# A recurrence with a max-out layer: weight differences made in pairs of chunks, lower_bound loaded on ScalarE's queue, and the last pair of blocks as seven products

## The chip, the cores and the metric

The kernel runs on one core of one Trainium2 chip. The metric is the device time of an execution in microseconds (us). The profile's span is about 1.8 us shorter than the time of the same run, and the text says which one it means.

## The reference, cut to what matters

A gated recurrence over 4 sequences of 6144 tokens of width 256 is followed by a two-layer network whose hidden unit is the larger of two projections:

```python
f = lower_bound + (1 - lower_bound) * sigmoid(f_logit)
h = f[:, t] * h + (1 - f[:, t]) * x[:, t]         # t = 0 .. 6143, y[:, t] = h
g = np.maximum(y @ w1, y @ w2)                    # width 1024
out = g @ w_out                                   # width 256
```

All inputs and the output are float32.

## The kernel before: the parts that matter here

The maximum is `y@w1 + relu(y@(w2-w1))`, so TensorE (PE) makes one product with `wd = w2 - w1` per hidden chunk and folds `w1 @ w_out` into a small matrix `w13`. Tokens are worked on in 48 blocks of 512. From block 4 on, the second layers of two blocks are made together as seven half-size products instead of eight (a Strassen scheme, with sums of activations made by VectorE). In the kernel before, the last pair of blocks is an exception: it still runs the plain second layer.

At the start, everything has to be built once. SyncE (SP) issues the loads in this order, and VectorE (DVE) casts what arrives:

```python
nc.sync.dma_start(out=lbc[:], in_=lower_bound.rearrange("(h p) -> p h", p=P))
nc.vector.tensor_copy(out=ident[:], in_=ident_f[:])
nc.vector.tensor_scalar(out=om[:], in0=lbc[:], scalar1=-1.0, scalar2=1.0, ...)   # 1 - lower_bound
nc.vector.tensor_scalar_add(out=nom[:], in0=lbc[:], scalar1=-1.0)
fetch_first(0)          # first 256 rows of f and of x
fetch_first(1)          # the next 256 rows of each
for g in range(NG):
    fetch_w(g)          # half of w1, half of w2, 512 KB each
pool_waits(w1n[0][:, 0, 0:1])      # GpSimd (POOL) waits for the first weight piece ...
nc.gpsimd.dma_start(out=wob[:]...) # ... then loads w_out and the next chunks of f and x, casting them
```

wd is made a half (four chunks) at a time, and the transposed w1 is copied out between the halves:

```python
scale_w1(0); half_w1(0, nc.scalar.copy)
make_wd(0)                 # DVE: wd = om * w2 - w1s, 2 x [128 x 512]
pt = turn_w1(0)            # PE: transpositions of w1
keep_w1T(0, pt)            # DVE copies them out of PSUM
scale_w1(1)
for fc in range(4):
    first_layer(0, fc)     # PE: needs wd of chunk fc
# ... the same for half 1, chunks 4..7 ...
make_w13(0)                # PE: needs both transposed halves and wob
```

The kernel's end is the plain second layer of the last two blocks, 80 matmuls of 256 columns, where each 128-token group of the last block is evicted and stored by itself.

## Time and profile before

| | before |
|---|---|
| median of the first 3 runs (lowest to highest) | 380.85 us (380.81 to 381.16) |
| profiled run | 381.55 us, span 379.8 us |
| busy share of the span | PE 97%, VectorE 88%, ScalarE 79% |
| 16 DMA engines, 3 to 22 us | 90% busy or more, one short stretch aside (80%) |

The page's first lines and its chain of waits (shares of the span by engine, then by line) are:

```profile
PE 369.1 (97%) x4076; PEld 279.9 (74%) x4076; DVE 333.0 (88%) x402; ACT 300.3 (79%) x406; POOL 37.5 (10%) x79
...
PE 89%; DMA 4%; DVE 3%; POOL 1%; SPq 1%; ACT 0%; issue 0%
PE ps L605 42%; PE dT L436 41%; PE ps L482 6%; DMA xT<-in_x_dram 3%; DMA r<-in_moe_w_dram 1%; DVE r L230 1%; DVE S L506 1%; SPq L117 0%; PE ps L180 0%; DVE osb L496 0%; DVE v L223 0%; POOL fT L105 0%; DVE ff L213 0%; ACT r L444 0%; POOL wob L631 0%
```

PE is the limit nearly everywhere. The view of windows (stretch, its length, then busy us and instructions of each engine, the granted clock, the DMA share and GB/s) shows where it isn't:

```profile
0.00:12.50 12.50, 7.11 (x57) 5.60 (x57) 7.56 (x18) 7.38 (x12) 4.48 (x14) 1.00 0.84 266
...
67.00:350.00 283.00, 283.00 (x3310) 215.28 (x3309) 270.50 (x308) 239.19 (x328) 25.68 (x55) 1.00 1.02 211
350.00:366.90 16.90, 16.90 (x207) 13.15 (x205) 9.90 (x12) 12.28 (x15) 0.00 (x0) 1.00 0.16 64
366.90:380.00 13.10, 8.70 (x80) 7.71 (x78) 2.23 (x4) 1.33 (x3) 0.00 (x0) 1.00 0.42 162
```

From 67 to 366.9 us PE has no idle time at all. What PE does not fill lies in the first 25 us and in the last 13, but for 0.55 us between 25 and 67. The chain in order of time (start, length, what) shows what set PE's progress at the start, and the last pair at its end:

```profile
0.74 0.44 SPq L620
...
1.25 0.45 SPq L117
...
3.16 5.50 DMA r<-in_moe_w_dram
...
11.39 11.08 DMA xT<-in_x_dram
...
22.52 0.62 PE ps L180 x8
...
366.87 8.75 PE ps L482 x80
```

L620 is the load of lower_bound, L117 the first loads of f and x, `xT<-in_x_dram` is x of chunk 2 (counted from 0) by way of POOL, and L482 the plain second layer of the last pair.

### The profile page before, as it was taken

How to read it: one execution, taken by the hardware profiler on the slowest of the kernel's cores; microseconds unless marked ns; L12 is line 12 of the kernel's file. 1: busy time of each engine (PE TensorE's matmuls, PEld its weight loads, DVE VectorE, ACT ScalarE, POOL GpSimd, SP SyncE). 2: the span in 40 equal slices, each digit the busy share in tenths (PEclk: the TensorE clock that was granted, in tenths of full speed). 3: DMA queues.
4: the chain of work that ended last, by engine and by line, in shares of the span. 5: the costliest groups of instructions: out<-in, count | busy, mean ns of one | idle time of the engine just before them, and what ended most of it. 6: DMA issues, size and time to landing. Idle time of an engine off the chain costs nothing.

```text
span 379.8 us, 9454 instructions
## 1 busy us (share of the span) xinstructions
PE 369.1 (97%) x4076; PEld 279.9 (74%) x4076; DVE 333.0 (88%) x402; ACT 300.3 (79%) x406; POOL 37.5 (10%) x79
## 2 busy tenths in 40 slices
PE   4999999999999999999999999999999999999995
PEld 3677766777777777777777777777777777777784
DVE  4696789999999999999999999999999999999721
ACT  4846788798798888888888887987888888888740
POOL 1500103101201101102011011011011021000000
PEclk9999999999999999999999999999999999999999
DMA  7994999989999999999899999999999999970223
GB/s 249 242 226 98 265 162 256 167 156 289 195 195 276 180 190 251 202 172 285 143 257 190 219 251 278 127 263 223 182 263 212 188 268 211 192 265 3 110 113 113
DMA packets 103389, 77.17 MB, mean 203 GB/s; under 512 B 93554, under 2 KB 94066, under 8 KB 102642
## 3 DMA queue, kind: packets, MB, share of 16 engines
q1 hardware_dynamic: 100514, 51.13, 59.8%
q0 software_dynamic: 2544, 25.17, 34.5%
q8 instruction: 32, 0.52, 0.6%
q10 hardware_dynamic: 288, 0.26, 0.2%
q14 instruction: 11, 0.09, 0.1%
HBM read 53.48 MB, written 48.23 MB: 268 GB/s over the span
## 4 chain that ended last, share of the span: by engine, by line
PE 89%; DMA 4%; DVE 3%; POOL 1%; SPq 1%; ACT 0%; issue 0%
PE ps L605 42%; PE dT L436 41%; PE ps L482 6%; DMA xT<-in_x_dram 3%; DMA r<-in_moe_w_dram 1%; DVE r L230 1%; DVE S L506 1%; SPq L117 0%; PE ps L180 0%; DVE osb L496 0%; DVE v L223 0%; POOL fT L105 0%; DVE ff L213 0%; ACT r L444 0%; POOL wob L631 0%
## 5 line engine op out<-in xcount | busy, mean ns | idle before, releaser
L444 ACT ACTIVATE r<-dT 128x1024 f16<-128x1024 f32 x192 | 195.8, 1022 | 53.2 <-PE dT L436 53.0
L436 PE MATMUL dT<-r,wd 128*128 128x512 f16 x768 | 225.4, 379 | 1.0 <-DVE wd L360 0.5
L605 PEld LDWEIGHTS <-S 128*128 128x128 f16 x1680 | 110.9, 101 | 37.6 <-issue 0.6
L605 PEld LDWEIGHTS <-r 128*128 128x128 f16 x1260 | 87.3, 101 | 36.6
L230 DVE TENSOR_TENSOR_SCAN r<-ff,r,v 128x512 f16<-128x512 f16 x88 | 108.2, 1270 | 0.8
L605 PE MATMUL ps<-t,S 128*128 128x128 f16 x1260 | 97.8, 219 | 0.0
L436 PEld LDWEIGHTS <-wd 128*128 128x128 f16 x768 | 67.6, 113 | 6.4 <-DVE wd L360 1.1
L506 DVE TENSOR_TENSOR S<-r 128x2560 f16<-128x2560 f16 x42 | 62.4, 1485 | 10.1 <-ACT r L444 10.0
L605 PE MATMUL ps<-wob,r 128*128 128x128 f16 x672 | 67.4, 219 | 0.0
L506 DVE TENSOR_TENSOR S<-r,S 128x2560 f16<-128x2560 f16 x42 | 61.9, 1474 | 0.0
L285 ACT ACTIVATE u<-fT 128x512 f16<-128x512 f16 x88 | 56.0, 636 | 1.0 <-DMA fT<-scr 1.0
L213 DVE TENSOR_SCALAR ff<-u,nom 128x512 f16<-128x512 f16 (+1 forms) x98 | 31.3, 346 | 9.7 <-ACT u L207 5.3
L348 POOL CAST waited<-fT 128x1 f32<-128x1 f16 x21 | 10.8, 513 | 279.5 <-DMA fT<-scr 279.5
L605 PE MATMUL ps<-w,r 128*128 128x128 f16 x168 | 36.8, 219 | 0.0
L562 DVE TENSOR_TENSOR osb<-ps,sn 128x512 f32<-128x512 f32 x42 | 28.7, 684 | 6.8 <-ACT osb L560 5.3
L605 PE MATMUL ps<-t,r 128*128 128x128 f16 x420 | 33.4, 219 | 0.0
L605 PE MATMUL ps<-wob,S 128*128 128x128 f16 x336 | 31.4, 219 | 0.0
L223 DVE TENSOR_TENSOR v<-u,xT 128x1024 f16<-128x1024 f16 x44 | 30.1, 684 | 0.2 <-DMA xT<-scr 0.2
L482 PEld LDWEIGHTS <-r 128*128 128x128 f16 x240 | 23.9, 101 | 6.9
L482 PE MATMUL ps<-wob,r 128*128 128x256 f16 x192 | 26.8, 273 | 0.0
L550 ACT COPY sn<-ps 128x512 f32<-128x512 f32 x42 | 24.6, 587 | 1.1 <-PE ps L605 0.9
L560 ACT COPY osb<-ps 128x512 f32<-128x512 f32 x42 | 24.4, 582 | 0.5 <-PE ps L605 0.5
(56 smaller groups left out, 134.8 us busy)
## 6 DMA issues: line engine op xcount, KB each, us to landing
out_dram<-osb SPq DMA_DIRECT2D x47, 512.0 KB, 3.9
scr<-in_f_logit_dram POOLq DMA_DIRECT2D x22, 512.0 KB, 7.4
scr<-in_x_dram POOLq DMA_DIRECT2D x22, 512.0 KB, 10.4
r<-in_moe_w_dram SPq DMA_DIRECT2D x4, 512.0 KB, 6.8
fT<-in_f_logit_dram POOLq DMA_DIRECT2D x3, 256.0 KB, 9.2
xT<-in_x_dram POOLq DMA_DIRECT2D x3, 256.0 KB, 11.1
osb<-in_f_logit_dram SPq DMA_DIRECT2D x2, 256.0 KB, 4.5
osb<-in_x_dram SPq DMA_DIRECT2D x2, 256.0 KB, 4.1
```

What stands on the lines that cost most here:

```text
L213: nc.vector.tensor_scalar(out=ff[:, h, cols], in0=u[:, h, cols], scalar1=nom[:, h : h + 1], scalar2=1.0, op0=ALU.mult, op1=ALU.add,)
L223: nc.vector.tensor_tensor(out=like(v[:, :, cols], xT), in0=like(u[:, :, cols], xT), in1=xT, op=ALU.mult,)
L230: nc.vector.tensor_tensor_scan(out=y_of(j, h), data0=ff[:, h, o : o + TB], data1=v[:, h, o : o + TB], initial=0.0 if t0 == 0 else y_of(j - ...
L285: nc.scalar.activation(out=mids[p + NBLK, "u"][:, h, cols], in_=held[c, 0][:, h, cols], func=AF.Sigmoid, scale=-1.0,)
L436: nc.tensor.matmul(dT[:, fc % 2, :], lhsT=wd[:, kc, unit_cols(fc)], rhs=y_of(j, kc), start=(kc == 0), stop=(kc == KC - 1),)
L444: nc.scalar.activation(out=rts[j, k][:, g - 1 : g + 1, :].rearrange("p q (i m) -> p q i m", m=P), in_=dT[:].rearrange("p q (m i) -> p q i ...
L482: nc.tensor.matmul(ps[:, r, :], lhsT=left, rhs=right, start=(s == 0 and (r == 0 or j == NBLK - 1)), stop=(s == n - 1 and (r == 1 or j == N ...
L506: nc.vector.tensor_tensor(out=t[:], in0=a, in1=b, op=op)
L550: nc.scalar.copy(out=t[:], in_=bank[b][:])
L560: nc.scalar.copy(out=dst, in_=bank[b][:])
L562: nc.vector.tensor_tensor(out=dst, in0=bank[b][:], in1=snap[name][:], op=ALU.add)
L605: nc.tensor.matmul(bank[b][:, i, :], lhsT=a[:, k, cols], rhs=w, start=fresh, stop=after is not None, skip_group_check=True,)
```

## The change

Three parts, each meant to take something off an end of the kernel: wd is made for two chunks at a time, so that PE can begin the first layer sooner, and the copies of the transposed w1 move behind it; lower_bound is loaded on ScalarE's (ACT's) queue, so that SP's first load of f is issued sooner; and the last pair is made as seven products of 128 columns like all others, with its last product (the "M2" of the scheme) in two parts. With the second part go two small moves: ScalarE's first Sigmoid (`warm`) no longer needs lower_bound and runs earlier, and VectorE makes `nom` (lower_bound - 1) ahead of `om`. The core of the diff:

```diff
-    def make_wd(g):
+    def make_wd(g, pair):
+        def cut(t):
+            return t.rearrange("p (n q) -> p n q", q=NQ)[:, :, 2 * pair : 2 * pair + 2]
         for kc in range(KC):
             nc.vector.scalar_tensor_tensor(
-                out=wd[:, kc, g * NQ * P : (g + 1) * NQ * P],
-                in0=w2n[g][:, kc, :],
+                out=cut(wd[:, kc, g * NQ * P : (g + 1) * NQ * P]),
+                in0=cut(w2n[g][:, kc, :]),
 ...
-        nc.sync.dma_start(out=lbc[:], in_=lower_bound.rearrange("(h p) -> p h", p=P))
+        nc.scalar.dma_start(out=lbc[:], in_=lower_bound.rearrange("(h p) -> p h", p=P))
         nc.vector.tensor_copy(out=ident[:], in_=ident_f[:])
+        nc.scalar.activation(out=warm[:], in_=ident_f[:, 0:1], func=AF.Sigmoid)
+        nc.vector.tensor_scalar_add(out=nom[:], in0=lbc[:], scalar1=-1.0)
         nc.vector.tensor_scalar(out=om[:], in0=lbc[:], ...)
 ...
-        make_wd(0)
-        pt = turn_w1(0)
-        keep_w1T(0, pt)
         scale_w1(1)
-        for fc in range(4):
-            first_layer(0, fc)
+        pt0 = turn_w1(0)
+        for pair in range(2):
+            make_wd(0, pair)
+            for fc in range(2 * pair, 2 * pair + 2):
+                first_layer(0, fc)
 ...                                  # the same for half 1, then:
+        keep_w1T(0, pt0)
+        keep_w1T(1, pt1)
 ...                                  # the end: sum3 in the last round, then
-        for j in (NBLK - 2, NBLK - 1):
-            for slot in range(FC):
-                second_layer(j, slot)
+        sum1(p); sum2(p); sum4(p)
+        for step in sevenths(p):
+            step()
 ...                                  # in sevenths, for the last pair:
+            product("X", sub(3), given(t3))
+            then(leave_both("X"))    # DVE evicts X; ACT saves group 3 of X
+            product("E", sub(4), plain(1, hi))
+            then(leave("E", ja, hi, 2, True))
+            product("X", part(1, 1), given(t4), groups=range(3))
+            then(leave_last(slice(0, 3)))
+            product("Y", part(1, 1), given(t4), True, groups=range(3, 4))
+            then(leave_last(slice(3, 4)))
```

In the last pair every finished half (128 of the 256 columns) is stored at once, so a store there writes runs of 512 B, where the stores before wrote whole rows of 1 KB or four rows of 1 KB in one run.

More of the change, by code (lines that the diff above doesn't have):

```diff
@@ L356, in half_w1 @@
             copy(out=w1h[g][:, kc, :], in_=w1s[g][:, kc, :])
-    def make_wd(g):
+    def make_wd(g, pair):
+        def cut(t):
+            return t.rearrange("p (n q) -> p n q", q=NQ)[:, :, 2 * pair : 2 * pair + 2]
         for kc in range(KC):
             nc.vector.scalar_tensor_tensor(
-                out=wd[:, kc, g * NQ * P : (g + 1) * NQ * P],
-                in0=w2n[g][:, kc, :],
+                out=cut(wd[:, kc, g * NQ * P : (g + 1) * NQ * P]),
+                in0=cut(w2n[g][:, kc, :]),
                 scalar=om[:, kc : kc + 1],
-                in1=w1s[g][:, kc, :],
+                in1=cut(w1s[g][:, kc, :]),
                 op0=ALU.mult,
@@ L450, in first_layer, with store @@
             )
-    def store(j, osb, first=0, n=TB // P, queue=None):
+    def store(j, osb, groups=slice(0, TB // P), cols=slice(0, D), queue=None):
         b, t0, nb, c, o = blocks[j]
@@ L456, in store @@
             out=out[r0 : r0 + nb, :].rearrange("(p n) d -> p n d", p=P)[
-                :, first : first + n, :
+                :, groups, cols
             ],
-            in_=osb[:, first : first + n, :],
+            in_=osb[:, groups, cols],
         )
@@ L470, in second_layer @@
             g, r = divmod(i, 2)
-            if s == 0 and (r == 0 or j == NBLK - 1):
+            if s == 0 and r == 0:
                 acc["ps"] = ps_o.tile([P, 2, D], FP32, name="ps")
@@ L485, in second_layer @@
                 rhs=right,
-                start=(s == 0 and (r == 0 or j == NBLK - 1)),
-                stop=(s == n - 1 and (r == 1 or j == NBLK - 1)),
+                start=(s == 0 and r == 0),
+                stop=(s == n - 1 and r == 1),
                 skip_group_check=True,
             )
-            if j == NBLK - 1 and s == n - 1:
-                (nc.vector.tensor_copy if r else nc.scalar.copy)(
-                    out=osb[:, i : i + 1, :], in_=ps[:, r : r + 1, :]
-                )
-                store(j, osb, i, 1, nc.sync if r else nc.scalar)
-            elif r == 1 and s == n - 1:
+            if r == 1 and s == n - 1:
                 (nc.scalar.copy if j == 0 else nc.vector.tensor_copy)(
@@ L528, in sevenths, with product, open_bank @@
         ja, jb = 2 * p, 2 * p + 1
-        def product(b, left, w, fresh=False):
-            for i in range(TB // P):
+        end = p == NPAIR - 1
+        def product(b, left, w, fresh=False, groups=range(TB // P)):
+            for i in groups:
                 for k in range(KH + 1):
-                    steps.append([b, left, w(k), i, k, fresh and i == k == 0, None])
+                    new = fresh and i == groups[0] and k == 0
+                    steps.append([b, left, w(k), i, k, new, None])
         def then(fn):
             steps[-1][-1] = fn
-        def open_bank(b):
-            bank[b] = ps_o.tile([P, TB // P, P], FP32, name="ps")
+        def open_bank(b, i=0):
+            if i:
+                t = ps_d.tile([P, 2 * TB // P, P], FP32, name="dT")
+            else:
+                t = ps_o.tile([P, TB // P, P], FP32, name="ps")
+            bank[b] = t
         def seed(b, src):
@@ L564, in go, with leave_both, leave_last @@
                     )
-                if last:
+                if end:
+                    store(j, osbs[j], cols=cols)
+                elif last:
                     store(j, osbs[j])
+            return go
+        def leave_both(b):
+            def go():
+                leave(b, jb, hi, 5, False)()
+                t = snpool.tile([P, TB // P, P], FP32, name="sn")
+                nc.scalar.copy(out=t[:, 3, :], in_=bank[b][:, 3, :])
+                snap[4] = t
+            return go
+        def leave_last(at):
+            def go():
+                dst = osbs[jb][:, at, lo]
+                if at.start:
+                    nc.vector.tensor_tensor(
+                        out=dst, in0=bank["Y"][:, at, :], in1=snap[4][:, at, :],
+                        op=ALU.add,
+                    )
+                else:
+                    nc.scalar.copy(out=dst, in_=bank["X"][:, at, :])
+                store(jb, osbs[jb], at, lo, nc.sync if at.start else nc.scalar)
             return go
@@ L585, in sevenths @@
         then(snapshot("E", 5))
-        product("X", sub(2), given(t2))
-        then(snapshot("X", 2))
-        product("B", part(0, 1), plain(1, lo))
-        then(leave("B", ja, lo, None, False))
-        product("X", sub(3), given(t3))
-        then(leave("X", jb, hi, 5, False))
-        product("E", sub(4), plain(1, hi))
-        then(leave("E", ja, hi, 2, True))
-        product("X", part(1, 1), given(t4))
-        then(leave("X", jb, lo, None, True))
+        if end:
+            product("B", part(0, 1), plain(1, lo), groups=range(1))
+            product("X", sub(2), given(t2))
+            then(snapshot("X", 2))
+            product("B", part(0, 1), plain(1, lo), groups=range(1, 4))
+            then(leave("B", ja, lo, None, False))
+            product("X", sub(3), given(t3))
[6 more added lines that the diff above has]
+            then(leave_last(slice(3, 4)))
+        else:
+            product("X", sub(2), given(t2))
+            then(snapshot("X", 2))
+            product("B", part(0, 1), plain(1, lo))
+            then(leave("B", ja, lo, None, False))
+            product("X", sub(3), given(t3))
+            then(leave("X", jb, hi, 5, False))
+            product("E", sub(4), plain(1, hi))
+            then(leave("E", ja, hi, 2, True))
+            product("X", part(1, 1), given(t4))
+            then(leave("X", jb, lo, None, True))
         def runner(step):
@@ L601, in run @@
                 if fresh:
-                    open_bank(b)
+                    open_bank(b, i)
                 a = left()
@@ L624 @@
         )
-        nc.vector.tensor_scalar_add(out=nom[:], in0=lbc[:], scalar1=-1.0)
         fetch_first(0)
@@ L637 @@
                 fetch(c, s)
-        nc.scalar.activation(out=warm[:], in_=om[:, 0:1], func=AF.Sigmoid)
         wt = ps_d.tile([P, 2, 2 * TB], HALF, name="dT")
@@ L653 @@
         half_w1(0, nc.scalar.copy)
-        make_wd(0)
-        pt = turn_w1(0)
-        keep_w1T(0, pt)
         scale_w1(1)
-        for fc in range(4):
-            first_layer(0, fc)
-        half_w1(1, nc.vector.tensor_copy)
-        make_wd(1)
-        pt = turn_w1(1)
-        for fc in range(4, 8):
-            first_layer(0, fc)
-        keep_w1T(1, pt)
+        pt0 = turn_w1(0)
[3 more added lines that the diff above has]
+                first_layer(0, fc)
+        half_w1(1, nc.vector.tensor_copy)
+        pt1 = turn_w1(1)
+        for pair in range(2):
+            make_wd(1, pair)
+            for fc in range(4 + 2 * pair, 6 + 2 * pair):
+                first_layer(0, fc)
+        keep_w1T(0, pt0)
+        keep_w1T(1, pt1)
         steps = turn_steps(1)
@@ L715 @@
             more = p + 1 < NPAIR
-            seq = [(27, scans[p]["scan10"]), (36, scans[p]["scan11"])]
+            seq = [
+                (27, scans[p]["scan10"]),
+                (36, scans[p]["scan11"]),
+                (112, lambda: sum3(p)),
+            ]
             if more:
@@ L723 @@
                     (84, scans[p + 1]["scan01"]),
-                    (112, lambda: sum3(p)),
                     (131, scans[p + 1]["decay1"]),
@@ L753 @@
             step()
-        for j in (NBLK - 2, NBLK - 1):
-            for slot in range(FC):
-                second_layer(j, slot)
+        p = NPAIR - 1
+        sum1(p)
+        sum2(p)
+        sum4(p)
+        for step in sevenths(p):
+            step()
 _INS = ['x', 'f_logit', 'lower_bound', 'moe_w1', 'moe_w2', 'moe_w_out']
```

## The prediction

> **What bounds the kernel now.** The page gives PE 97% busy; the chain of waits puts 89% of the span on PE. The windows view has PE busy for all of 67 to 366.9 us, which the change doesn't touch. So the change is worth what its two ends are worth, out of 10.7 us that PE doesn't fill.
>
> **Start.** The chain of waits: from 0.74 us SP issues lower_bound (0.44 us), four 256 KB loads (0.45 us each), then the weights; the first weight piece lands at 8.66 and lets POOL issue; x of the third chunk lands at 22.47, and PE goes on at 22.52. The DMA view shows the 16 engines 90% busy or more from about 3 to 22 us (370 to 400 GB/s on weights, 205 on POOL's casting loads): a stream of fixed length that begins when SP gets to its first load.
> - lower_bound on ScalarE's queue takes 0.51 us from the front (1.25 to 0.74): the stream ends about 0.45 us earlier. The Trainium skill, "DMA: Bandwidth & Descriptors", section "Issuing engines are not separate DMA queues", says that another issuer saves issue time only; that is what is wanted here.
> - wd in pairs: wd takes 1.39 us per half on DVE, and the weight loads idle 0.55 us twice behind it. Pairs and a later keep_w1T (0.68 us) should end block 0's first layer near 15.6 instead of 16.83, but wob lands near 16.5 and that x at 22.47, so PE will wait longer there (0.3 to about 1 us). I give this part nothing of its own.
> From 51.4 to 64 us the chain is on DVE, but it starts from a PE result and moves along.
>
> **End.** The last pair is 80 matmuls of 256 columns, 8.75 us (109 ns each) after 366.87. Seven products are 140 of 128 columns at 55.5 ns (27 took 1.51 us): 7.8 us. The last relu ends at 366.42; a sum takes 1.48 us (1.40 pipelined), so sum1 is ready at 368.0, just when product 1 ends, sum2 at 369.4, sum4 at 370.8. PE should end near 374.75, not 375.61. The last eviction is 128x128, about 0.3 us against 0.42. Stores become half rows of 512 B: packets took 45 ns for 1 KB, 84 for 2, 159 for 4, so I estimate 26 ns; the same page (Specifications) puts the line-rate minimum at 512 B, so no collapse. The last two stores (256 KB) need about 0.8 us of engines from 375.8, against 0.5 us from 376.9. Last byte about 376.65 against 377.4: 0.75 us gained. The 2.4 us from there to the end of the span stay.
>
> **Sum.** 0.45 + 0.75 = 1.2 us: 379.6 us, range 379.0 to 380.3. Chances: faster by over 2% 0.01, within 2% 0.98, slower 0.01.
>
> **Right or wrong.** Right if the first load is issued at about 0.74; x of chunk 2 lands about 0.5 us earlier; PE waits for it about 1 us, is busy from there to about 1.3 us before its old end, and shows no gap over 0.1 us in the last products; 512 B packets take about 26 ns.
>
> **What would make it wrong.** lower_bound's 4-byte packets still delaying the first load; the table load behind ScalarE's issue delaying the first sigmoid; 512 B packets as slow as 1 KB ones, or half-row stores issuing slower than 0.33 us; sums late on DVE; strided wd halves costing clearly more than half.

## The result, and the profile after

| | before | after |
|---|---|---|
| median (lowest to highest), 4 runs each | 380.83 us (380.80 to 381.16) | 380.18 us (380.08 to 380.82) |
| ratio of the fast runs | | 0.9985, 95% interval 0.9967 to 1.0002 |
| span of the profiled run | 379.8 us | 378.5 us |

Ratios here are the mean time of one kernel's fast runs over that of the other's of the same rounds, so they are not quite the ratio of the medians. The medians differ by 0.65 us. The forecast was 379.6 us with a range of 379.0 to 380.3, so the range holds, but the gain is about half of the 1.2 us that I summed up. The two spans differ by 1.3 us, which looks like my sum; but the span of before came from a slow draw. Against a second profile of the kernel before (b_again below, span 378.97 us) the change's 378.50 is 0.47 us shorter: 0.39 of it before the first layer of block 1, 0.08 from the last pair on.

The page after:

```profile
PE 367.7 (97%) x4136; PEld 279.2 (74%) x4136; DVE 338.4 (89%) x409; ACT 302.4 (80%) x410; POOL 36.2 (10%) x79
...
PE 92%; DVE 5%; DMA 1%; ACT 0%; issue 0%; DVEq 0%
```

The chain after, in order of time:

```profile
0.74 3.87 DMA lbc<-in_lower_bound_dram
4.63 0.17 DVE nom L667
...
4.87 0.34 DVE nat L128
...
11.32 0.39 DVE wd L365
11.75 2.10 PE dT L441 x8
```

This is not the chain I had forecast. The stream of loads is gone from it. It now begins with lower_bound itself, which takes 3.87 us to land, and VectorE's first cast of f (L128) stands behind the two operations on it. From there it runs over VectorE to wd and on to PE. The wait for x of chunk 2, which should have grown to 1 us, isn't there at all.

The end, as the timeline of the kernel before and that of the kernel after show it (start, length, engine, line, operation; in brackets the idle time before it and what ended it). Before:

```profile
374.57 1.04 PE L482 MATMUL ps<-wob,r 128*128 128x256 f16 x8
...
375.64 0.42 DVE L491 COPY osb<-ps 128x256 f32<-128x256 f32 x1 [1.76 <-PE ps L482]
```

After:

```profile
366.82 1.13 PEld L649 LDWEIGHTS <-S 128*128 128x128 f16 x20 [0.17 <-DVE S L506]
...
372.37 0.22 PE L649 MATMUL ps<-w,S 128*128 128x128 f16 x1
...
372.61 1.00 PE L649 MATMUL ps<-t,r 128*128 128x128 f16 x15
...
373.44 0.44 PE L649 MATMUL dT<-t,r 128*128 128x128 f16 x5
...
373.99 0.29 DVE L589 TENSOR_TENSOR osb<-dT,sn 128x128 f32<-128x128 f32 x1 [0.68 <-PE dT L649]
374.15 0.43 ACTq L460 DMA_DIRECT2D out_dram<-osb  x1
```

From the start of the last pair's first matmul to the end of the last, PE took 8.90 us before (366.71 to 375.61) and 8.36 after (365.52 to 373.88): 0.54 us gained, not 0.86. Two gaps of 0.18 us show: before the second product, which waits for sum1, and before the last, where the starts of two neighbouring matmuls are 0.24 us apart instead of 0.056, because VectorE (until 372.25 us) and then ScalarE (until 372.56) first have to read the bank that it adds to.

### The profile page after: what moved, and what is told of

The parts are those of the page before. It is cut to its first block, busy times and chain, and to the rows that moved or that the text cites. A ratio compares the mean times of both kernels' runs of the same rounds, so it can differ in the third digit from the quotient of the medians.

```text
span 378.5 us, 9591 instructions
## 1 busy us (share of the span) xinstructions
PE 367.7 (97%) x4136; PEld 279.2 (74%) x4136; DVE 338.4 (89%) x409; ACT 302.4 (80%) x410; POOL 36.2 (10%) x79
## 4 chain that ended last, share of the span: by engine, by line
PE 92%; DVE 5%; DMA 1%; ACT 0%; issue 0%; DVEq 0%
PE ps L649 45%; PE dT L441 42%; PE ps L487 4%; DVE r L230 1%; DVE S L506 1%; DMA lbc<-in_lower_bound_dram 1%; PE ps L180 1%; DVE v L223 1%; DVE r L264 1%; DVE ff L213 0%; PE ps L397 0%; DVE osb L496 0%; ACT r L449 0%; PE ps L137 0%; ACT u L258 0%
## 5 line engine op out<-in xcount | busy, mean ns | idle before, releaser
L649 PEld LDWEIGHTS <-S 128*128 128x128 f16 x1760 | 115.4, 101 | 37.8 <-issue 0.6
L649 PEld LDWEIGHTS <-r 128*128 128x128 f16 x1320 | 90.9, 101 | 36.7
L649 PE MATMUL ps<-t,S 128*128 128x128 f16 x1320 | 101.6, 219 | 0.0
L506 DVE TENSOR_TENSOR S<-r 128x2560 f16<-128x2560 f16 x44 | 65.4, 1487 | 14.4 <-ACT r L449 14.3
L649 PE MATMUL ps<-wob,r 128*128 128x128 f16 x704 | 69.9, 219 | 0.0
L506 DVE TENSOR_TENSOR S<-r,S 128x2560 f16<-128x2560 f16 x44 | 65.0, 1478 | 0.0
L649 PE MATMUL ps<-w,r 128*128 128x128 f16 x176 | 38.5, 219 | 0.0
L348 POOL CAST waited<-fT 128x1 f32<-128x1 f16 x21 | 9.4, 449 | 280.6 <-DMA fT<-scr 280.6
L568 DVE TENSOR_TENSOR osb<-ps,sn 128x512 f32<-128x512 f32 x44 | 30.1, 685 | 3.2 <-PE ps L649 3.2
L487 PEld LDWEIGHTS <-r 128*128 128x128 f16 x160 | 16.0, 101 | 6.2
L649 PE MATMUL ps<-w,S 128*128 128x128 f16 x88 | 19.3, 219 | 0.0
```

What stands on the lines that cost most here:

```text
L487: nc.tensor.matmul(ps[:, r, :], lhsT=left, rhs=right, start=(s == 0 and r == 0), stop=(s == n - 1 and r == 1), skip_group_check=True,)
L506: nc.vector.tensor_tensor(out=t[:], in0=a, in1=b, op=op)
L568: nc.vector.tensor_tensor(out=dst, in0=bank[b][:], in1=snap[name][:], op=ALU.add)
L649: nc.tensor.matmul(bank[b][:, i, :], lhsT=a[:, k, cols], rhs=w, start=fresh, stop=after is not None, skip_group_check=True,)
```

## The experiments

Twelve kernels were run, in three groups of four. Each was timed against the kernel before in the same rounds, and each left a profile. Each group ran on another chip, so times are set against the kernel before of their own rounds. All gave correct results.

One reading of the profiles orders everything. Let "first layer of block 1" be the start of PE's first matmul of that stage. From there to the first matmul of the last pair it is 341.54 or 341.55 us in ten of these profiles with the stage order unchanged and one core clock, before or after, whichever parts they have. The window view shows the same stretch with the same PE busy time. The kernel before (its second profile, b_again):

```profile
24.40:365.90 341.50, 340.95 (x3830) 257.04 (x3828) 314.54 (x368) 284.67 (x382) 34.07 (x61) 1.00 0.96 201
```

The kernel after:

```profile
24.00:365.50 341.50, 340.95 (x3830) 257.02 (x3828) 316.18 (x370) 284.48 (x382) 28.63 (x61) 1.00 0.96 202
```

So a span is the start, plus 341.55, plus the end, and each part of the change can be read from two numbers. This table is worked out from the profiles' instruction and packet times (us):

```
profile     1st decay  wd starts  w13 starts  1st layer  last pair to  span
            on DVE     on DVE     on PE       block 1    end of span
before      5.76       11.09      16.67       25.16      13.06         379.77
b_again     5.77       10.78      16.36       24.36      13.06         378.97
lb_only     6.34       11.03      16.61       24.62      13.11         379.26
wd_only     5.81       10.61      15.40       23.43      13.06         378.03
tail_only   5.86       10.75      16.57       24.90      12.96         379.40
after       6.53       11.23      15.94       23.97      12.98         378.50
no_lb       5.84       10.89      15.60       24.22      12.96         378.72
nom_late    6.20       11.03      16.25       24.65      12.96         379.16
full_rows   6.34       11.04      15.75       23.78      13.02         378.35
lb_rows     5.28       10.45      17.70       25.70      12.99         380.24
turn_late   5.81       10.86      16.13       24.14      12.96         378.77
rows_late   5.33       10.76      16.34       24.41      13.01         379.08
rows_gate   5.33       10.44      15.49       23.89      12.99         378.87
```

And the times:

| run | parts | median (lowest to highest) | ratio to before | 95% interval |
|---|---|---|---|---|
| after | all three | 380.18 (380.08 to 380.82) | 0.9985 | 0.9967 to 1.0002 |
| b_again | none | 380.76 (380.66 to 381.14) | 0.9995 | 0.9982 to 1.0008 |
| lb_only | lower_bound | 381.14 (380.98 to 381.38) | 1.0003 | 0.9990 to 1.0016 |
| wd_only | wd in pairs | 380.60 (379.81 to 380.98) | 0.9985 | 0.9972 to 0.9999 |
| tail_only | seven products | 380.80 (380.49 to 381.44) | 0.9995 | 0.9982 to 1.0009 |
| no_lb | wd and seven products | 379.96 (379.66 to 380.53) | 0.9975 | 0.9961 to 0.9988 |
| nom_late | all, VectorE reordered | 380.32 (379.78 to 380.94) | 0.9984 | 0.9970 to 0.9999 |
| full_rows | all, whole-row stores | 380.63 (380.13 to 381.15) | 0.9993 | 0.9978 to 1.0008 |
| lb_rows | all, lower_bound as rows | 381.27 (379.07 to 382.27) | 0.9999 | 0.9974 to 1.0025 |
| turn_late | no_lb, one stage moved | 380.83 (379.88 to 382.41) | 1.0001 | 0.9984 to 1.0018 |
| rows_late | lb_rows, one stage moved | 380.86 (380.12 to 381.26) | 0.9997 | 0.9984 to 1.0010 |
| rows_gate | rows_late, POOL later | 380.58 (379.92 to 380.65) | 0.9987 | 0.9975 to 0.9999 |

lb_third isn't in the tables; it stands below. The kernel before ran 42 times in all, its first profiled run not counted: median 380.85, 380.52 to 382.35, 8 of 10 between 380.64 and 381.36. Differences of a few tenths are therefore read from the profiles, and the times are only asked whether they agree. A profile is one draw too: after and full_rows have the same start, word for word, and their wd starts 0.19 us apart (11.23 and 11.04).

### The kernel before, profiled again (b_again)

No edit. Theory A held that the first profile had been a slow draw; the rival was that the change made POOL's loads faster.

> The kernel before, unchanged, for a second profile. The profiled run of before was 0.7 us over that kernel's median, and there POOL's loads of the start were slow (the wob load was waited for until 16.53 us, against 14.84 in the profile after). Theory A (that profile was a slow draw of the start): x of chunk 2 now lands before about 21.9 us, PE doesn't wait for it, and PE reaches the last pair's products about 0.7 us earlier, near 366.2 us instead of 366.87. Rival B (the change itself made POOL's loads faster): x of chunk 2 lands near 22.5 us again. Ratio 1.000 either way.

PE's transposition of x of chunk 2 began at 21.74 us without a wait, and the last pair at 365.91. Theory A holds: this profile is 0.8 us shorter than the first one of the same kernel, all of it before block 1's first layer. Its chain at the start does not run over the stream at all:

```profile
2.21 4.17 DMA osb<-in_f_logit_dram
...
10.14 0.73 DVE r L264
10.87 1.31 DVE wd L360 x2
12.17 0.60 DVE w1T L384
12.77 0.67 DVE S L356 x2
13.44 1.33 DVE wd L360 x2
14.82 1.70 PE dT L436 x7
16.52 0.87 PE ps L392 x8
```

In this execution, whose time is at the kernel's median, the start is a chain on VectorE: the first recurrence, the first half of wd, the copy of the transposed w1 (L384), a cast, and the second half of wd, with PE behind. That copy and those halves are what the wd part of the change cuts.

### lower_bound alone (lb_only)

```diff
-        nc.sync.dma_start(out=lbc[:], in_=lower_bound...)
+        nc.scalar.dma_start(out=lbc[:], in_=lower_bound...)
+        nc.scalar.activation(out=warm[:], in_=ident_f[:, 0:1], func=AF.Sigmoid)   # was behind om
         # nom ahead of om
```

> Only lower_bound on ScalarE's queue (with the early warm-up and nom ahead of om). My prediction's step: SP's stream starts 0.51 us earlier and PE with it: 0.45 us faster. Theory A: VectorE, in order, waits for lower_bound until about 4.6 us because its 4-byte packets now share the engines with the 2 KB packets of the first loads, so the first cast starts at about 4.8 us instead of 4.0 and the first recurrence ends no earlier: within 0.2 us of before, or slower by up to 0.5.

It gained nothing: 381.14 us at the median against 380.75 for before in the same rounds, with an interval that holds 1. VectorE in b_again:

```profile
2.88 0.17 DVE L622 TENSOR_SCALAR om<-lbc 128x2 f32<-128x2 f32 x1 [1.31 <-DMA lbc<-in_lower_bound_dram]
...
5.77 0.48 DVE L213 TENSOR_SCALAR ff<-u,nom 128x256 f16<-128x256 f16 x2
```

VectorE in lb_only:

```profile
4.44 0.17 DVE L623 TENSOR_SCALAR nom<-lbc 128x2 f32<-128x2 f32 x1 [2.88 <-DMA lbc<-in_lower_bound_dram]
...
6.34 0.48 DVE L213 TENSOR_SCALAR ff<-u,nom 128x256 f16<-128x256 f16 x2 [0.78 <-ACT u L258]
```

lower_bound lands 1.56 us later than when it goes first on SP, although it is issued at the same 0.74 us. The first decay starts 0.57 us later and wd 0.25 us later. Theory A holds. One step of my prediction also holds: the first piece of the weights does land earlier. POOL sees the first weight piece landed at 8.15 to 8.30 us in the four profiles with lower_bound on ScalarE's queue as 4-byte packets, and at 8.43 to 8.89 in the six with it first on SP. It did not help here, because VectorE's chain, which starts from f and x, was the longer one.

The packets of the trace say why lower_bound lands late. Counted from them, in each quarter of a microsecond: KB of f, x and weights whose transfer started, and the number of 4-byte packets (lower_bound is 256 of them; the rest are semaphores):

```
from us   b_again       after         lb_rows
1.75        0 KB  59     26 KB   0     28 KB   0
2.25        8 KB  96     38 KB   0     52 KB   0
2.75       46 KB   0     54 KB  43     92 KB   5
3.00       84 KB   0     30 KB  65     96 KB   5
3.25       92 KB   4     14 KB  82     94 KB   4
3.50       60 KB  12     18 KB  36     70 KB  10
3.75       54 KB   0     18 KB  21     70 KB   2
4.00       84 KB   3     12 KB  39     54 KB   6
4.25       74 KB   8     84 KB   2     40 KB   3
```

First on SP, lower_bound's packets run at a time when the engines have nothing else: the first of them starts at 1.82 us in b_again. On ScalarE's queue the first one starts at 2.82 us (2.49 to 2.82 in the four profiles with it there, though it is issued as early), which is part of the late landing and stays unexplained. From then on they run beside the first loads, and from 3.0 to 4.25 us the loads start 92 KB (128 to 162 in the other three) where b_again's start 374. The 0.5 us of head start is spent there. The Trainium skill, "DMA: Bandwidth & Descriptors", section "Queues, rings and completion order", says that each engine takes turns between the queue rows that have work; that fits packets of two queues mixing for a whole microsecond, but by the packets' own durations (9 ns) they should have cost little.

### wd in pairs alone (wd_only)

The edit is the `make_wd` part of the diff above with the order of the calls, and nothing else.

> Only wd in pairs of chunks, with keep_w1T behind. My prediction's step: nothing, PE waits longer for x of chunk 2. Theory A: in a usual run that x lands early enough, so that the first layer of block 0 ends about 1.0 us earlier and PE reaches the second layer 0.7 to 1.1 us earlier: 0.6 to 1.1 us faster.

The profile agrees with Theory A (0.93 us at block 1's first layer), but it is that of the fastest of the six runs (379.81), set against a median run of b_again. The ratio, 0.9985, is that of the whole change: about 0.57 us, with an interval from 0.04 to 1.07. The median of the runs moved only 0.15 us. PE in b_again:

```profile
11.57 2.37 PE L436 MATMUL dT<-r,wd 128*128 128x512 f16 x8
...
14.22 0.38 PE L436 MATMUL dT<-r,wd 128*128 128x512 f16 x1
14.82 1.70 PE L436 MATMUL dT<-r,wd 128*128 128x512 f16 x7 [0.23 <-DVE wd L360]
16.36 1.04 PE L392 MATMUL ps<-wob,w1T 128*128 128x256 f16 x8
```

PE in wd_only:

```profile
11.38 1.89 PE L441 MATMUL dT<-r,wd 128*128 128x512 f16 x8
...
13.55 2.01 PE L441 MATMUL dT<-r,wd 128*128 128x512 f16 x8
15.40 1.06 PE L397 MATMUL ps<-wob,w1T 128*128 128x256 f16 x8
```

The cleanest measure is the distance from the first wd operation to the first product of w13 (L392, L397), because it leaves out when the first loads came. It is 5.58 us in before, b_again and lb_only, and 4.79, 4.71, 4.71 and 4.71 in wd_only, after, no_lb and full_rows: 0.8 to 0.9 us. In the other profiles it is longer, and the gain is in part waited away: with pairs 5.05 in rows_gate, 5.22 in nom_late, 5.27 in turn_late, 5.58 in rows_late and 7.25 in lb_rows, and without them 5.82 in tail_only. Two reasons show in the traces: w1 turned late (tail_only's first layer began 1.25 us after wd, b_again's 0.79) and TensorE at full rate late (see lb_rows below). A third, wob late, is likely in nom_late: the product, which reads wob, began 0.28 us behind its turn there, and POOL saw wob land at 16.49. I had given this part nothing. It is where the gain of the start comes from.

### The last pair as seven products alone (tail_only)

The edit is the part of the diff from `store` to `sevenths`, with the last lines of the kernel.

> Only the last pair as seven products, with half-row stores. My prediction's step: 0.75 us faster. Theory A, from the profile after: PE ends the last pair in 8.2 us instead of 8.74 (0.54 gained, with two gaps of 0.18 us), but from the end of PE to the end of the span it takes 4.6 us instead of 4.2: 0.0 to 0.2 us faster.

From the last pair's first matmul to the end of the span it took 12.96 us, against 13.06: 0.1 us, as Theory A had it, and no measurable time (380.80 against 380.75). PE's gain of half a microsecond is given back behind PE. In b_again the last byte is written 2.11 us after the last matmul starts, in after 2.84 us. Counted from the last pair's first matmul, the last byte even comes later than before: 10.98 us in after and 10.97 here, 10.72 in before and b_again. That the span still ends 0.1 us sooner is due to the time behind the last byte, which I can't explain (full_rows below). The DMA view of the end lists the stores (line, queue, count, size, median us from issue to landing); before (b_again):

```profile
out_dram<-osb ACTq DMA_DIRECT2D x2, 128.0 KB, 2.5
out_dram<-osb SPq DMA_DIRECT2D x2, 128.0 KB, 2.1
```

After:

```profile
out_dram<-osb SPq DMA_DIRECT2D x3, 256.0 KB, 2.6
out_dram<-osb ACTq DMA_DIRECT2D x1, 192.0 KB, 2.8
out_dram<-osb SPq DMA_DIRECT2D x1, 64.0 KB, 2.4
```

The packets of 512 B took 25 to 26 ns, as I had estimated from the three larger sizes in the trace of the kernel before. But the store with 512 of them took 1.29 us from issue to its first packet where the engines were idle (371.05 to 372.34), and I had reckoned with the 0.80 of a store with 128. The five stores of the last pair then follow each other almost without a pause, from 372.34 to 376.50.

### The change without lower_bound's part (no_lb)

```diff
-        nc.scalar.dma_start(out=lbc[:], in_=lower_bound...)
+        nc.sync.dma_start(out=lbc[:], in_=lower_bound...)     # first, as before; warm and om as before
```

> The change without its lower_bound part: wd in pairs and the seven products, lower_bound first on SP again. Theory A (wd pairs gain about 0.6 to 0.9 us, the tail about 0.1, lower_bound on ScalarE's queue loses about 0.3): 0.7 to 1.0 us faster than before, and 0.2 to 0.4 faster than the whole change; PE reaches the last pair near 365.0 us instead of 365.5. Rival (the gain of the whole change needs the earlier first load): no faster than the whole change.

379.96 us at the median, 0.90 below before in the same rounds, ratio 0.9975 with an interval that ends at 0.9988. It is the fastest of the kernels by median, and the only one whose interval lies clearly below 1. Its profile is that of its slowest run (380.53): PE waited for x of chunk 2 there,

```profile
21.58 0.62 PE L180 MATMUL ps<-ident,xT 128*128 128x128 f16 x8 [0.42 <-DMA xT<-in_x_dram]
```

so that the last pair came at 365.77 and not near 365.0; that number of Theory A missed in this draw. Against the whole change the runs are 0.2 us better at the median (379.96 and 380.18), but from other rounds and with overlapping intervals, so it is shown only that the lower_bound part isn't needed for the gain.

### VectorE doesn't wait for lower_bound (nom_late)

```diff
-        nc.vector.tensor_scalar_add(out=nom[:], in0=lbc[:], ...)   # and om
         ...
         first_bf16(0, 0, nc.vector.tensor_copy)
         first_bf16(0, 1, nc.vector.tensor_copy)
+        nc.vector.tensor_scalar_add(out=nom[:], in0=lbc[:], ...)   # and om
```

The Trainium skill, "TensorE: Matmul & The Clock Gate", gives VectorE's queue as strictly first in, first out (its table of specifications), and the chain after shows it: the cast of f stands behind nom. This run asks how much that wait costs by itself.

> The whole change, with VectorE's two operations on lower_bound put behind its first two casts. It keeps the slowed stream (the 4-byte packets among the 2 KB packets from 3 to 4 us) and takes away VectorE's in-order wait for lower_bound. If that wait is what costs: the first cast starts near 4.2 us instead of 4.8, the first decay near 5.9 instead of 6.5, PE reaches the last pair 0.4 to 0.6 us earlier than the whole change. If the slowed stream is what costs: the second cast still waits for x until about 5.4 us and PE gains under 0.2 us.

The first cast moved to 4.18 us, as expected of the wait, but the cast of x still waited for its data until 5.58, as expected of the slowed stream. The first decay came at 6.20 (after: 6.53, b_again: 5.77) and wd at 11.03 (11.23 and 10.78). So the slowed stream is what costs most. What the wait in order adds is not settled: full_rows keeps it and drew 6.34 and 11.04, so between nothing and 0.2 us is left at wd. The time, 380.32, is that of the whole change; wob landed late in this draw.

### lower_bound without 4-byte packets (lb_rows)

```diff
-        nc.scalar.dma_start(out=lbc[:], in_=lower_bound.rearrange("(h p) -> p h", p=P))
+        nc.scalar.dma_start(out=lbr[:], in_=lower_bound.rearrange("(h p) -> h p", p=P))   # 2 rows of 512 B
 ...
+        nc.tensor.transpose(lbt[:], lbr[:], ident_f[0:KC, 0:KC])
+        # nom and om from lbt, behind the two casts
```

> The whole change, with lower_bound loaded as two rows of 512 B on ScalarE's queue, turned by one fp32 transposition on PE, and nom and om made behind the first two casts. No 4-byte packets are left in the start. If these slowed the stream: from 3 to 4 us the engines start over 80 KB per 0.25 us instead of 14 to 30, f lands before 3.6 us and x near 4.7 instead of 5.4, and PE reaches the last pair 0.3 to 0.6 us earlier than with lower_bound first on SP (no_lb): 1.0 to 1.5 us faster than before. If not: x lands near 5.2 us again and the result is that of no_lb.

The cause was hit and the gain was not. With two packets in place of 256 the loads run at 92 to 96 KB per quarter microsecond from 2.75 to 3.5 us (the table above), f is cast at 3.52 and x at 4.14 us, and the first decay starts at 5.28, half a microsecond ahead of b_again. That settles that the 4-byte packets slowed the stream. But the runs went from 379.07, the fastest of all, to 382.27, and the profile, taken of a slow one (382.05), shows the weights late. ScalarE in lb_rows:

```profile
9.01 1.34 ACT L352 ACTIVATE r<-r,om 128x512 f32<-128x512 f32 x2 [1.11 <-DMA r<-in_moe_w_dram]
10.26 1.13 ACT L356 CAST S<-r 128x512 f16<-128x512 f32 x2
```

The scaling of w1 (L352) had to wait 1.11 us for its data; in after it starts at 8.22 without a wait. PE turns w1 before it begins the first layer, so in this draw the first layer waited for w1 (ScalarE's casts, done at 11.4 us) and not for wd, which had started at 10.45. A second chain, weights to ScalarE to PE, lies close behind the VectorE chain, and shortening one by half a microsecond brings up the other.

That is only half of this draw's loss. The first layer of block 0 also ran slowly. PE in lb_rows:

```profile
12.16 3.52 PE L441 MATMUL dT<-r,wd 128*128 128x512 f16 x8
...
15.97 1.89 PE L441 MATMUL dT<-r,wd 128*128 128x512 f16 x8
```

The first eight matmuls start 0.427 us apart, the next eight 0.216, the same form with no wait between them. The trace's record of the clock that TensorE is granted, at its full share (1.0), begins at 15.46 us here, just where the spacing halves; in the other twelve profiles of the table it begins between 9.37 and 13.20. From the first layer's first matmul to w13 it took 5.54 us, against 4.02 in wd_only (lines above): 1.5 us of TensorE's rate, beside about 1 us of waiting for w1. The same shows in smaller measure in rows_late (about 0.75 us, full rate at 13.20), and in nom_late and turn_late (0.3 to 0.4 us, at 12.59 and 12.61). Why the full rate came late in these draws is not shown, nor whether it spreads the runs that left no trace.

### lower_bound third on SP's own queue (lb_third)

As nom_late, with lower_bound issued by SP between the first x and the second f.

> As nom_late, but lower_bound is issued on SP, third, behind the first f and x, so that its 4-byte packets share a ring with the 2 KB packets and not a second ring beside it. Theory A1 (4-byte packets cost wherever they run beside loads): the engines start under 40 KB per 0.25 us for about 1 us again, x lands near 5.2 us or later. Theory A2 (only the turn-taking between two rings costs): the 4-byte packets pass in a burst behind x, f lands near 3.5 us and x near 4.2, the first decay starts near 5.3 us, and the second halves of f and x land about 0.5 us later than in nom_late or the same.

The profile fell in the slow state (granted clock 0.95 from 11.07 us on, where its record begins), so only its first microseconds are used. f was cast at 3.63, x at 4.30, and the first decay started at 5.38 us: Theory A2. The 4-byte packets passed in a burst, 253 of them from 3.5 to 4.0 us. The place mattered: on the same queue behind x they delay neither f nor x. But the second halves of f and x came later (second decay at 8.98 us, 8.63 in nom_late), and the fast runs lay between 379.66 and 382.09 us: no gain.

### Whole rows at the end (full_rows)

```diff
-                if end:
-                    store(j, osbs[j], cols=cols)
-                elif last:
+                if last:
                     store(j, osbs[j])
 ...
-                store(jb, osbs[jb], at, lo, ...)
+                store(jb, osbs[jb], at, ...)          # groups 0 to 2 and group 3, all 256 columns
```

> The whole change, with the last pair stored in whole rows: the first block of the pair at once behind its last product, the second in one piece of 3 KB and one of 1 KB per partition. In the profile after, a half-row store of 3 or 4 pieces per partition takes 1.26 to 1.29 us from issue to its first byte, against 0.80 for one piece. Theory A: these take 0.80 us again, but 0.5 MB more waits for the end, so that the last byte is within 0.3 us of the whole change's and the time is the same. My prediction's step (half rows carry less at the end and cost nothing else): 0.4 to 0.6 us slower than the whole change.

Both expectations are half right. The first store's first packet came 0.83 us after its issue again (373.19 to 374.02), but the last two waited behind it, and the last byte came 11.51 us after the last pair's first matmul, against 10.98 in after: 0.53 later, as my prediction's reckoning of bytes has it. Yet the span ended 13.02 us after that matmul, against 12.98. So the form of the stores is worth 0.04 us in these two profiles, and the time from the last byte to the end is not fixed, as I had assumed: 2.3 us in before, 2.0 in after, 1.5 here. What sets it stays open.

### Three attempts to make the start robust (turn_late, rows_late, rows_gate)

```diff
         for fc in range(FC):
-            if fc == 4:
-                turn(turn_steps(2))
-                gate(2)
             second_layer(0, fc)
+        turn(turn_steps(2))
+        gate(2)
-        pool_waits(w1n[0][:, 0, 0:1])          # rows_gate only
+        pool_waits(w2n[0][:, 0, 0:1])
```

turn_late is no_lb with this move, rows_late lb_rows with it, and rows_gate adds the later start of POOL.

> As no_lb (wd in pairs, seven products, lower_bound first on SP), with the transpositions of block 2 moved behind the whole second layer of block 0, 2.2 us of PE later. In no_lb's profile PE waited for x of chunk 2 (0.42 us, until 21.58) in that draw. If POOL's late landings are what spreads the runs: no wait for that x in any draw, PE reaches the last pair at 365.0 us or earlier, median 0.2 to 0.5 us below no_lb's and a narrower spread. If the order costs VectorE its slack: the scans of block 2 start about 1.4 us later and PE waits for them at the first layer of block 2, no gain.

> As lb_rows (lower_bound as two 512 B rows), with block 2's transpositions moved as in turn_late. lb_rows ran between 379.07 and 382.27; its profile was a slow draw (382.05) in which f and x were ready 0.5 to 1.0 us early, but the weights came late: from 10.5 to 11.8 us, when POOL's wob packets had begun, the engines started 12 to 68 KB per 0.25 us. If only the late x of chunk 2 cost it: 379.0 to 379.8 in every run. If the late weights cost it (PE's first layer of block 0): again runs over 381.

> As rows_late, with POOL's first load held back until the second weight piece has landed instead of the first, so that its packets meet less of the weights' stream. If that collision makes lb_rows's slow runs: no run over 380.5 us, the weights' last packets end by 12.0 us, and the median is near 379.3. If not: the same spread as lb_rows.

None beat no_lb. In its profile the move took away the wait for x of chunk 2, and it cost 0.12 us later (341.67 us in the middle). turn_late still spread from 379.88 to 382.41, so that wait is hardly what spreads the runs. rows_gate did part of what its theory expects: the weights' last packet ended at 11.71 us (12.03 in rows_late, 12.52 in lb_rows), no run was over 380.65 us, and w13 started at 15.49 in its profile, where TensorE was also at full rate by 11.43 us. But it lost 0.44 us in the middle (341.99), and its median is 380.58, not 379.3: holding POOL back gives the gain away again. Five runs don't show that it narrows the spread.

## Why the prediction was right or wrong

The range was right, and so was the statement that the change is worth what its two ends are worth: the middle is 341.54 to 341.55 us in all profiles that keep its order. But the sum was right only by errors that cancel.

- "A stream of fixed length that begins when SP gets to its first load ... the stream ends about 0.45 us earlier": this step failed. The first load was issued at 0.74 us as forecast, and the first weight piece did land earlier, by about 0.4 us. But lower_bound's packets, moved out of an empty stretch into the busy one, slowed f and x, and VectorE stood behind lower_bound; alone, this part put block 1's first layer 0.26 us later in the profile (a difference that two draws of one start can also have) and gained nothing in time. The prediction had named a delay by these packets among what would make it wrong, and given it no weight.
- "I give this part nothing of its own" (wd in pairs): this step failed, and it is the larger miss. The first layer of block 0 did end earlier (16.10 us in after and 15.56 in wd_only instead of 16.83; forecast 15.6). But the wait for x that should have swallowed the gain came with slow executions: of the profiles with the stage order unchanged, only before and no_lb show it (0.30 and 0.42 us), and no_lb's is its slowest run. I had read one profile as the kernel, though its run was 0.7 us over the median. Where that x, wob, w1 and TensorE's full rate come early, VectorE's chain over wd sets the start, and the part shortens it by 0.8 to 0.9 us; over all runs of wd_only the time fell by about 0.57.
- "0.75 us gained" (the end): it measured 0.1 us. On PE the mechanism was right and the term mis-sized: 0.54 instead of 0.86, for two gaps of 0.18 us that I had forecast as none over 0.1. Behind PE the step failed: two of the last pair's stores took 1.29 and 1.26 us from issue to first byte and the last one 1.44, instead of 0.80, and queued behind each other, so that the last byte came 0.26 us later after the pair's first matmul, not 0.75 earlier. That 0.1 us is left is luck: "the 2.4 us from there to the end" became 2.0. The 512 B packets took the 26 ns that I had estimated.
- Not settled: the spread of the starts. POOL saw wob land either near 15 us (14.84 to 15.26 in six profiles) or near 16.5 (16.29 to 16.74 in five), with two before, between or beyond, and the weights' landing moved by up to 0.9 us. The kernels with a part of the change and those without both show both cases. TensorE's full rate began anywhere from 9.37 to 15.46 us, which alone cost 1.5 us in lb_rows's profile. Why any of these moves is open.

## What to carry to other kernels

When a profiled run is slower than the median of the timed runs by as much as the effect that you forecast, take a second profile before reasoning about its waits: the wait at the end of a chain may be that draw's alone. A tiny strided load is not free because it is tiny; put it where the engines have nothing else, or load it in rows and turn it on chip (which kept the loads fast here, though it brought no gain in time). When one kernel's runs spread, compare the spacing of equal matmuls at its start: TensorE may be running at half its rate (0.427 us against 0.216 here), which is no wait and shows as busy time. At the end of a kernel, count what is behind the last matmul (eviction, issue, packets, landing) with the same care as the matmuls, since a gain on PE of half a microsecond came to a tenth.

## What the Trainium skill lacked or had wrong

- "DMA: Bandwidth & Descriptors", "Issuing engines are not separate DMA queues", says that another issuing engine only saves issue time. It lacks the cost: 256 packets of 4 bytes on ScalarE's queue beside SP's 2 KB packets cut the loads to 92 to 162 KB in 1.25 us, against 374 KB in b_again, though each packet is recorded with 9 ns. The page warns of small transfers elsewhere, and its section "Queues, rings and completion order" explains the mixing, but neither gives this price to the loads beside them.
- The same page, "Specifications", gives 512 B as the smallest transfer for line rate. Here 512 B packets of stores took 25 to 26 ns and 4 KB packets 159 ns, which I estimate as 320 and 412 GB/s over 16 engines that never pause (512 B / 25.6 ns x 16, and 4096 B / 159 ns x 16): 78% of the rate.
- The same page, "Latency and other measured facts", gives about 600 ns to HWDGE's first byte. From the start of the issuing instruction to the first packet, with the engines idle, it was 0.83 us for a store of 128 packets and 1.29 us for one of 512. No page gives it by the number of packets.
- No page mentions how much the landing of a core's first loads varies from run to run: the same kernel's wob load was seen landed at 14.99 and at 16.53 us in two profiles of the kernel before.
